# A scale column made by two-column matmuls, and transposes moved ahead of it, in front of a V projection

## The chip, the cores and the metric

The kernel runs on one core of a Trainium2 chip. The metric is the device time of one execution in microseconds (us). The profile's span, from the first to the last profiled instruction, is 1.8 to 2.3 us shorter than that time; what lies outside it varies from run to run.

## The reference

The kernel is the attention half of a two-stream transformer block: batch 2, 256 image and 32 text tokens, width 1152. What matters here is the way to the image stream's V:

```python
mod_i = (silu(c) @ wmod_img).reshape(B, 6, 1, D)
shi, sci, gai = mod_i[:, 0], mod_i[:, 1], mod_i[:, 2]
hi = layernorm(x_img) * (1 + sci) + shi
qkvi = hi @ wqkv_img            # q, k, v of the image stream
# ... text stream, softmax attention, output projections, gates ...
```

The kernel applies the scale `1 + sci` first, computes V from the scaled input and adds the shift's share later. So before the first V matmul it needs normalised x, transposed (contraction on the partitions), and the scale as a column per 128 channels. The 256 image tokens of a batch are two token tiles of 128: tiles 0 and 1 of batch 0, 2 and 3 of batch 1.

## The kernel before

The contraction is cut into nine blocks of 128 (`kt` 0 to 8). The scale needs all nine rows of blocks of its weights, which arrive in four transfers (kt 0-3, 4-6, 7, 8), before any column of it is complete. The code is cut, and the arguments of DVE's instructions are shortened.

```python
def sc_rows(r0, r1):            # scale as rows: silu(c) is stationary, weights stream
    ...                         # r0 == 0: the constant 1, by `unit` and `warm`
    for kt in range(r0, r1):
        for g in range(NGG):    # four column tiles of the array side by side
            mm(sc_ps[LW*g:LW*g+LW], lhsT=sT32[:, kt, :], rhs=group(w_sc_i, kt, g),
               start=False, stop=(kt == KT-1), tile_position=(0, LW*g))

def sc_cols(c0, c1):            # rows to columns: a transpose on DVE
    nc.vector.transpose(sc1_i[:, c0:c1, :], sc_ps[:, c0:c1, :])

def x_scale(k0, k1, b, step=TPB):   # hS = xT * column, on DVE
    ...

# the order in front of V (cut)
for out in [x_transposes(k0, 0) for k0 in (0, 3, 6)]:
    out()                       # batch 0: transpose on TensorE, copy out of PSUM
sc_rows(0, 4)
warm_up(3)
sc_rows(4, 7)
out01 = x_transposes(0, 1)      # batch 1, channel groups 0 and 3
out31 = x_transposes(3, 1)
sc_rows(7, K8)
sc_rows(K8, KT)
out61 = x_transposes(6, 1)      # group 6
out01()
sc_cols(0, 1)
x_scale(0, 1, 0, step=1)
sc_cols(1, 5)
x_scale(1, 3, 0)
v_open(A0, 0, 3)                # the first V matmuls
```

Two pools of PSUM, into which the kernel's matmuls write, matter. A pool hands out its banks in turn, and a tile that gets a used bank waits until the earlier contents have been read. `ps_tr` has two banks for transposes: groups 0 and 3 of batch 0 take them first, and groups 0 and 3 of batch 1 need the same two again. `ps_mm` has six.

## Time and profile before

| | kernel before |
|---|---|
| time, median of the first 3 runs | 118.11 us |
| span of the profiled run | 116.0 us |
| TensorE busy | 95% of the span |
| first V matmul starts | 14.15 us |
| from there to the end | 101.85 us |

The page's first part gives busy time by engine, the chain of work that ended last tells what the end waited for, step by step back to the start, and the timeline gives start and duration of each group. A bracket at the end of a timeline row gives the engine's idle time before it and what ended that. A landing is the moment at which a transfer's data have arrived. The prediction shows the lines and reads them.

### The profile page before, as it was taken

Reading aid. Unit: us, or ns where it says so; the run is one execution under the profiler, and the core shown is the slowest. Engines: PE = TensorE matmul, PEld = TensorE weight load, DVE = VectorE, ACT = ScalarE, POOL = GpSimd, SP = SyncE. Lnnn points to the kernel's source line nnn. Section 1 sums busy time; section 2 is a strip of 40 time slices with the busy share of each in tenths; the row PEclk is TensorE's granted clock in tenths of the full one; section 3 lists DMA queues with packets and bytes.
Section 4 is the critical chain, followed back from the end, with each engine's and each line's share of the span. In section 5 each row is a group of like instructions: output and inputs, shape, how many; then the busy total and the mean of one; then the engine's idle time right before and its main releaser. Section 6 shows DMA issues by size and latency. Waiting matters only on the chain.

```text
span 116.0 us, 2561 instructions
## 1 busy us (share of the span) xinstructions
PE 110.5 (95%) x1064; PEld 63.6 (55%) x1072; DVE 72.2 (62%) x153; ACT 44.3 (38%) x92; POOL 12.4 (11%) x34
## 2 busy tenths in 40 slices
PE   4999999999999999999999999999999999999990
PEld 1246644445674444444454457887866565566670
DVE  3478594062869999999995040018758508566571
ACT  4799710041752298725241233244657400100000
POOL 7300000000000000000000000003440700407000
PEclk9999999999999999999999999999999999999999
DMA  3999999999999999999999999999999999931323
GB/s 111 373 373 404 406 405 408 416 411 408 416 398 408 319 408 410 405 412 412 411 340 412 412 412 414 402 416 400 412 403 409 409 415 366 363 139 37 116 51 102
DMA packets 18917, 41.02 MB, mean 354 GB/s; under 512 B 1323, under 2 KB 1851, under 8 KB 18907
## 3 DMA queue, kind: packets, MB, share of 16 engines
q1 hardware_dynamic: 18032, 39.85, 89.4%
q0 software_dynamic: 480, 0.89, 2.3%
q10 hardware_dynamic: 395, 0.12, 0.4%
q8 instruction: 8, 0.13, 0.4%
q14 instruction: 2, 0.02, 0.0%
HBM read 39.52 MB, written 1.34 MB: 352 GB/s over the span
## 4 chain that ended last, share of the span: by engine, by line
PE 84%; DMA 8%; DVE 2%; SPq 1%; issue 1%; ACT 1%; DVEq 0%
PE ps L61 52%; PE vps L61 15%; DMA t<-in_wmod_img_dram 8%; PE gps L61 5%; PE aps L61 5%; PE sps L61 4%; DVE tmp L701 1%; PE sc_ps L61 1%; DVE o L702 1%; SPq L104 1%; PE tp L64 1%; ACT pT L621 1%; PE pT_ps L64 0%; SPq L108 0%; PE tpt L64 0%
## 5 line engine op out<-in xcount | busy, mean ns | idle before, releaser
L61 PE MATMUL ps<-xT_i,t 128*128 128x512 bf16 x157 | 35.4, 379 | 0.3
L61 PEld LDWEIGHTS <-t 128*128 128x128 bf16 x324 | 20.5, 98 | 19.0 <-issue 0.5
L435 DVE SCALAR_TENSOR_TENSOR acc_sh<-t,sTf,acc_sh 128x1152 f32<-128x1152 bf16 x16 | 21.4, 1404 | 0.0
L61 PE MATMUL ps<-t,aT 128*128 128x384 bf16 (+3 forms) x153 | 20.3, 308 | 0.0
L61 PE MATMUL vps<-t,hS_i 128*128 128x512 bf16 (+1 forms) x106 | 17.8, 325 | 0.2
L61 PEld LDWEIGHTS <-aT 128*128 128x128 bf16 (+1 forms) x153 | 13.0, 101 | 7.1 <-issue 0.8
L61 PEld LDWEIGHTS <-hS_i 128*128 128x128 bf16 x108 | 9.0, 98 | 8.7 <-DVE hS_i L264 0.4
L365 ACT CAST qkT<-ps 128x512 bf16<-128x512 f32 (+2 forms) x11 | 6.1, 551 | 15.0 <-PE ps L61 13.6
L701 DVE TENSOR_TENSOR tmp<-ps,gb 128x384 bf16<-128x384 f32 (+2 forms) x13 | 6.8, 524 | 7.2 <-DMA gb<-mod_scratch 3.8
L587 POOL TENSOR_SCALAR pb<-e,rs 128x32 bf16<-128x32 f32 (+1 forms) x5 | 2.2, 445 | 76.0 <-DVE rs L584 76.0
L61 PE MATMUL wps<-warm 128*128 128x512 bf16 x24 | 8.1, 499 | 1.6 <-DVE unit L127 1.5
L363 ACT ACTIVATE qkT<-ps 128x512 bf16<-128x512 f32 (+2 forms) x11 | 6.1, 561 | 8.6 <-PE ps L61 8.5
L180 DVE CAST v_i<-vps 128x512 bf16<-128x512 f32 x5 | 3.5, 691 | 7.5 <-PE vps L61 7.5
L572 DVE TENSOR_REDUCE nmx<-sps 128x1 f32<-128x288 f32 x4 | 1.8, 458 | 9.5 <-PE sps L61 9.5
L182 ACT CAST v_i<-vps 128x512 bf16<-128x512 f32 x4 | 2.3, 580 | 9.9 <-PE vps L61 9.9
L61 PEld LDWEIGHTS <-sT 128*32 128x32 bf16 x180 | 4.6, 96 | 2.4 <-issue 1.8
L61 PEld LDWEIGHTS <-warm 128*128 128x128 bf16 x25 | 2.7, 118 | 5.5 <-issue 3.0
L634 DVE TENSOR_SCALAR aT<-aps,svc 128x288 bf16<-128x288 f32 x9 | 4.3, 518 | 2.2 <-PE aps L61 2.2
L61 PE MATMUL sps<-qkT 128*128 128x288 bf16 (+1 forms) x54 | 5.3, 287 | 0.0
L61 PE MATMUL gps<-t,sT 128*32 128x288 bf16 x144 | 5.2, 287 | 0.0
L61 PE MATMUL ps<-hT_t,t 128*128 128x64 bf16 x162 | 5.2, 193 | 0.0
L61 PE MATMUL aps<-pT,v_i 128*128 128x288 bf16 x36 | 5.1, 287 | 0.1
(111 smaller groups left out, 105.3 us busy)
## 6 DMA issues: line engine op xcount, KB each, us to landing
t<-in_wqkv_txt_dram SPq DMA_DIRECT2D x3, 2592.0 KB, 19.1
t<-in_wmod_img_dram SPq DMA_DIRECT2D x2, 2592.0 KB, 14.1
t<-in_wmod_txt_dram SPq DMA_DIRECT2D x2, 2592.0 KB, 18.1
t<-in_wqkv_img_dram SPq DMA_DIRECT2D x3, 864.0 KB, 14.0
t<-in_wqkv_img_dram SPq DMA_DIRECT2D x1, 2592.0 KB
t<-in_wo_img_dram SPq DMA_DIRECT2D x3, 864.0 KB, 9.8
t<-in_wqkv_img_dram SPq DMA_DIRECT2D x3, 576.0 KB, 10.0
t<-in_wmod_txt_dram SPq DMA_DIRECT2D x2, 864.0 KB, 13.1
```

Source lines behind the costliest of these rows:

```text
L61: return pin(nc.tensor.matmul(*a, **k))
L64: return pin(nc.tensor.transpose(*a, **k))
L104: nc.sync.dma_start(x_i[:, b * TPB:(b + 1) * TPB, :], x_img[b].rearrange("(p t) d -> p t d", t=TPB))
L180: nc.vector.tensor_copy(out_ap, in_ap)
L182: nc.scalar.copy(out_ap, in_ap)
L363: nc.scalar.mul(out_ap, in_ap, SCALE)
L365: nc.scalar.copy(out_ap, in_ap)
L435: pin(nc.vector.scalar_tensor_tensor(acc, w_sh_t[:, kt, :], col, acc, op0=ALU.mult, op1=ALU.add))
L572: pin(nc.vector.reduce_max(nmx[0:qn, :], sps[0:qn, :], axis=AX.X, negate=True))
L587: pin(nc.gpsimd.tensor_scalar(pb[0:qn, NI + 2 * NT:NI + 3 * NT], e[0:qn, NI:NTOK], rs[0:qn, :], 0.0, op0=ALU.mult, op1=ALU.add))
L634: nc.vector.tensor_scalar(dst, tiles[(b, dt)][:], bias, None, op0=ALU.add)
L701: nc.vector.tensor_mul(tmp[:, 0:n], ps[:, 0:n], gb[:, b, c0:c0 + n])
```

## The change

The intent: the first block's scale column shouldn't have to go through rows and a DVE transpose. With the weights as the stationary operand, nine matmuls of two columns make it in place in PSUM, and DVE multiplies straight from there. The transposes of batch 1 are started earlier, by token tile, and the k0 = 6 groups of both batches have banks reserved. The diff is cut at the marks.

```diff
+    sc0_ps = ps_mm.tile([P, B], f32, tag="mm")
+    tp60 = ps_mm.tile([P, 3, NI], bf, tag="mm", name="tp")
+    tp61 = ps_mm.tile([P, 3, NI], bf, tag="mm", name="tp")
     sc_ps = ps_mm.tile([P, KT, LW], f32, tag="mm")
+    def sc_first(r0, r1):
+        if r0 == 0:
+            mm(sc0_ps[:], lhsT=warm[:, 0:P], rhs=unit[:, 0:B], start=True, stop=False)
+        for kt in range(r0, r1):
+            mm(sc0_ps[:], lhsT=w_sc_i[:, kt, 0:P], rhs=sT[:, kt, :], start=False, stop=(kt == KT - 1))
...
+    def x_tiles(k0, b):
+        return (tp61 if b else tp60) if k0 == 6 else ps_tr.tile([P, 3, NI], bf, tag="tr", name="tp")
...
...
     sc_rows(0, 4)
-    warm_up(3)
+    sc_first(0, 4)
+    warm_up(2)
+    t0, t3, t6 = [(x_tiles(k0, 1), k0, 1) for k0 in (0, 3, 6)]
+    x_transposes(*t0, ts=(1,))
+    x_transposes(*t3, ts=(1,))
     sc_rows(4, 7)
-    out01 = x_transposes(0, 1)
-    out31 = x_transposes(3, 1)
-    sc_rows(7, K8)
-    sc_rows(K8, KT)
-    out61 = x_transposes(6, 1)
-    out01()
-    sc_cols(0, 1)
-    x_scale(0, 1, 0, step=1)
-    sc_cols(1, 5)
+    sc_first(4, 7)
+    x_transposes(*t0, ts=(0,))
+    x_transposes(*t3, ts=(0,))
+    x_transposes(*t6)
+    sc_first(7, K8)
+    sc_first(K8, KT)
+    sc_rows(7, KT)
+    x_out(*t0)
+    x_out(*t6)
+    x_scale(0, 1, 0, step=1, first=True)
+    sc_cols(0, 5)
     x_scale(1, 3, 0)
     v_open(A0, 0, 3)
...
```

More of the change, by code (lines that the diff above doesn't have):

```diff
@@ L238, in sc_rows, with x_transposes, x_out @@
                    start=False, stop=(kt == KT - 1), tile_position=(0, LW * g))
-    def x_transposes(k0, b):
-        tr_pool = b == 1 or k0 < 6
-        tp = (ps_tr if tr_pool else ps_mm).tile([P, 3, NI], bf, tag="tr" if tr_pool else "mm", name="tp")
+    def x_tiles(k0, b):
+        return (tp61 if b else tp60) if k0 == 6 else ps_tr.tile([P, 3, NI], bf, tag="tr", name="tp")
+    def x_transposes(tp, k0, b, ts=range(TPB)):
         for kt in range(k0, k0 + 3):
-            for t in range(TPB):
+            for t in ts:
                 i = b * TPB + t
                 tr(tp[:, kt - k0, t * P:(t + 1) * P], xn_i[:, i, kt * P:(kt + 1) * P], ident[:])
+    def x_out(tp, k0, b):
         dst = xT_i[:, k0:k0 + 3, b * NI:(b + 1) * NI]
-        def copy_out():
-            pin(nc.vector.tensor_copy(dst, tp[:]) if k0 == 3 else nc.scalar.copy(dst, tp[:]))
-        return copy_out
+        pin(nc.vector.tensor_copy(dst, tp[:]) if k0 == 3 else nc.scalar.copy(dst, tp[:]))
     sc1_i = const.tile([P, KT, LW], f32, name="scc", tag="scc")
@@ L258, in sc_cols, with x_scale @@
                                 sc_ps[:, c0:c1, :].rearrange("p c l -> p (c l)")))
-    def x_scale(k0, k1, b, step=TPB):
+    def x_scale(k0, k1, b, step=TPB, first=False):
         for kt in range(k0, k1):
@@ L263, in x_scale @@
                 t0, t1 = b * NI + t * P, b * NI + (t + step) * P
-                pin(nc.vector.tensor_scalar(hS_i[:, kt, t0:t1], xT_i[:, kt, t0:t1], sc1_i[:, kt, b:b + 1], None,
+                pin(nc.vector.tensor_scalar(hS_i[:, kt, t0:t1], xT_i[:, kt, t0:t1],
+                                            sc0_ps[:, b:b + 1] if first else sc1_i[:, kt, b:b + 1], None,
                                             op0=ALU.mult))
@@ L302 @@
     ln_norm(x_i[:, 2, :], s2[:, 0:1], r2, P, xn_i[:, 2, :])
-    for out in [x_transposes(k0, 0) for k0 in (0, 3, 6)]:
-        out()
-    sc_rows(0, 4)
-    warm_up(3)
-    sc_rows(4, 7)
-    out01 = x_transposes(0, 1)
-    out31 = x_transposes(3, 1)
-    sc_rows(7, K8)
-    sc_rows(K8, KT)
-    out61 = x_transposes(6, 1)
-    out01()
-    sc_cols(0, 1)
-    x_scale(0, 1, 0, step=1)
-    sc_cols(1, 5)
+    tps = [(x_tiles(k0, 0), k0, 0) for k0 in (0, 3, 6)]
+    for tp in tps:
+        x_transposes(*tp)
+    for tp in tps:
+        x_out(*tp)
+    sc_rows(0, 4)
+    sc_first(0, 4)
[3 more added lines that the diff above has]
+    x_transposes(*t3, ts=(1,))
+    sc_rows(4, 7)
+    sc_first(4, 7)
[9 more added lines that the diff above has]
+    sc_cols(0, 5)
     x_scale(1, 3, 0)
     v_open(A0, 0, 3)
-    out31()
-    out61()
+    x_out(*t3)
     x_scale(0, 3, 1)
```

## The prediction

> **What bounds the kernel now.** I read the page's busy shares first, then the chain of work that ended last, then the timeline of the start, engine by engine.
>
> From the page of the kernel before:
>
> ```profile
> PE 110.5 (95%) x1064; PEld 63.6 (55%) x1072; DVE 72.2 (62%) x153; ACT 44.3 (38%) x92; POOL 12.4 (11%) x34
> ...
> PEclk9999999999999999999999999999999999999999
> ...
> PE 84%; DMA 8%; DVE 2%; SPq 1%; issue 1%; ACT 1%; DVEq 0%
> ```
>
> TensorE is busy 95% of the span at full clock and holds 84% of the chain. The chain in order of time shows where it is not yet the bound:
>
> ```profile
> 2.12 9.54 DMA t<-in_wmod_img_dram
> ...
> 11.70 0.55 PE sc_ps L61 x12
> 12.25 0.78 PE tp L64 x12
> 13.03 0.46 PE sc_ps L61 x8
> ...
> 13.51 0.23 DVE scc L257
> ...
> 13.83 0.27 DVE hS_i L264
> ...
> 14.15 2.12 PE vps L61 x9
> ```
>
> Until 11.7 us the start waits for the scale weights. Then come the last scale rows, the transposes of batch 1, the scale column made by DVE, the first scaled block, and at 14.15 us the first V matmul. From there to 111.4 us the chain is TensorE throughout, but for 0.65 us of one ScalarE copy and gaps of about 0.05 us (some of those are lost records: the spacing there is twice the usual 0.216 us). So the time follows the start of the first V matmul, one to one. Everything that the change touches lies in front of it.
>
> The parts of the timeline that I use, TensorE first (start, duration, both us):
>
> ```profile
> 10.10 0.66 PE L61 MATMUL sc_ps<-t,sT 128*32 128x288 bf16 x16
> ...
> 10.92 0.59 PE L61 MATMUL wps<-warm 128*128 128x512 bf16 x2 [0.16 <-issue]
> 11.70 0.55 PE L61 MATMUL sc_ps<-t,sT 128*32 128x288 bf16 x12 [0.18 <-DMA t<-in_wmod_img_dram]
> 12.19 0.84 PE L64 MATMUL tp<-ident,xn_i 128*128 128x128 bf16 x12
> 12.96 0.51 PE L61 MATMUL sc_ps<-t,sT 128*32 128x288 bf16 x8
> 13.58 0.49 PE L64 MATMUL tp<-ident,xn_i 128*128 128x128 bf16 x6
> ```
>
> ScalarE and DVE in the same stretch:
>
> ```profile
> 11.14 1.48 ACT L250 COPY xT_i<-tp 128x768 bf16<-128x768 bf16 x2
> ...
> 11.34 0.57 DVE L212 TENSOR_SCALAR xn_i<-x_i,sm,rstd 128x1152 bf16<-128x1152 bf16 x1
> 11.83 0.55 DVE L250 COPY xT_i<-tp 128x768 bf16<-128x768 bf16 x1
> 13.51 0.22 DVE L257 STREAM_TRANSPOSE scc<-sc_ps 128x32 f32<-128x32 f32 x1 [1.13 <-PE sc_ps L61]
> 13.83 0.42 DVE L264 TENSOR_SCALAR hS_i<-xT_i,scc 128x128 bf16<-128x128 bf16 x2
> ```
>
> The reader is to see three things. Transposes come every 0.056 us: (0.84 - 0.22) / 11. A group of four column-tiled row matmuls comes every 0.121 us (x16 are four groups). And the two banks of the transposing pool come free only when their batch-0 contents are copied out: the first at 11.14 + 0.78 = 11.92 us (ScalarE), the second at 11.83 + 0.55 = 12.38 us (DVE).
>
> **What the Trainium skill says.** "TensorEngine Tiling (Array Packing)", Key Properties: changing the tiling mode drains the engine. The trace agrees and gives the price: from the start of the last column-tiled matmul to the next full-width load it takes 0.21 us, where a group costs 0.12; from the last full-width transpose to the next column-tiled one 0.15 us, where a transpose costs 0.056. So about 0.09 us a switch. "TensorE: Matmul & The Clock Gate", Part 3, The mechanism: weight loads may be pulled ahead, matmuls keep their order. The trace agrees: the transposes at 13.58 us wait for ScalarE's third copy, and no matmul behind them passes. "VectorE: DVE Perf Modes", Why PSUM operands drop a tier: an operand in PSUM caps the DVE at its 2x mode. Whether that holds for a one-column scalar no row of the kernel before shows; it would turn 128 elements at 0.25 us into some 0.28 (estimate, from the 0.033 us that the trace has between the 128- and the 256-element scaling).
>
> **The change part by part.**
>
> *Removed:* the 32-column DVE transpose (0.22 us) and the wait between it and the scaling; 13.51 to 13.83 is 0.32 us of the chain. One of three warm-up matmuls (0.216 us) goes too, but it lay in front of a wait for weights.
>
> *Added:* ten matmuls of 2 columns (one for the constant, nine for the rows), each with a full load of 128 weights. The nearest thing in the trace is the text block's 128x64 matmul, also with a new load each: 33 take 1.12 us and one 0.193, so they start every 0.029 us and end 0.19 after their start. Ten cost 0.3 us of issue. The scale column for kt = 0 is ready 0.19 us after the last of them, instead of 0.30 + 0.32 after the last row group.
>
> *What the data allows:* the last row of scale weights is there at 13.13 us (its matmul starts at 13.157). Then 0.03 issue, 0.19 matmul, 0.05 signal, 0.27 scaling, 0.06 signal: V could start at 13.75. The first V weights, issued at 3.74 and landing 10.1 us later, come at 13.83. So the intent is worth at most 14.15 - 13.86 = 0.29 us, 0.25% of 118.1.
>
> *What the order makes of it:* the built program shows TensorE's new sequence: 16 row matmuls, 5 small, 2 warm-up, 3 transposes of token tile 3 into the first pool bank, **3 transposes of token tile 3 into the second pool bank**, 12 row matmuls (kt 4-6), 3 small, 12 transposes, 2 small, 8 row matmuls, V. The transposes come in front of the row matmuls now, and the second three still wait for DVE's copy that ends at 12.38. Only the k0 = 6 groups have banks of their own; the groups 0 and 3 do not. I step through it:
>
> - last of the 16 row matmuls starts 10.48; +0.21 switch: 10.70; 5 small to 10.85; 2 warm-up to 11.28.
> - token tile 3 is normalised at 11.43, but the first bank is free at 11.92, seen at 11.97: three transposes to 12.13.
> - second bank free at 12.38, seen at 12.44: three transposes, the last starts 12.55. In the kernel before, the 12 row matmuls had been issued by 12.09 and half of all transposes by this time.
> - +0.15 switch: 12.70, three groups, the last starts 12.95; +0.21: 13.16, 3 small to 13.25.
> - 12 transposes: 13.25 + 12 x 0.056 = 13.92.
> - 2 small at 13.92 and 13.95; their weights (12.4 and 13.13) are long there. The last ends at 14.14.
> - DVE: +0.04 signal, a second wait of some 0.07 (13.73 to 13.83 held such a pair): 14.25; scaling 0.25 to 0.30: 14.50 to 14.55; +0.06: **V at 14.56 to 14.61**, say 14.58.
>
> TensorE meanwhile: switch, 8 row matmuls from about 14.10, back in full mode by 14.42, so it then waits for DVE, not DVE for it.
>
> *Behind it:* DVE's transpose of five blocks is one instruction of about 0.34 us (32 columns take 0.22, 128 take 0.31). It starts at about 14.60, so the second scaled block is there at about 15.25, and V's second step needs it at 14.58 + 4 x 0.216 = 15.44. Batch 1 scales at about 15.9 to 16.5, needed at 14.58 + 12 x 0.216 = 17.2. V's weight blocks are all there before. So no new stall follows and the shift stays rigid: 14.58 - 14.15 = +0.43 us, and 118.11 + 0.43 = **118.5 us**.
>
> **The rivals.**
>
> 1. *The intent comes true:* V starts with its weights at 13.86, giving 117.8 us. For it: the removed DVE step really is in the chain. Against it: the column now waits for 12 transposes that used to be elsewhere, and for the second bank. It would need the three early transposes not to wait for 12.38. I give it about one chance in eight, or some middle result that cannot be told from no change.
> 2. *Clock:* TensorE idles from 11.28 to 11.97 and from 12.13 to 12.44 with one warm-up fewer. If the granted clock dropped, the next microseconds would run slower and the time would rise to 119.5 or more. Against it: the kernel before idles about as much in total between 11.3 and 14.15, in more pieces, and its clock row is full in every slice. About 4%.
> 3. *Hidden anyway:* later waits for weights could swallow the shift. Against it: the chain has no transfer after 11.66 us. If it held, 118.1.
> 4. *DVE becomes the bound:* a scalar read from PSUM makes both halves slow, say 0.4 us each. V would start 0.1 to 0.15 later, 118.7.
>
> **Range and chances.** The steps carry an error of some 0.15 us, mostly in the signals and in the scaling from PSUM; runs of the kernel before spread over 117.92 to 118.4. So 118.1 to 118.9 should hold it 8 times in 10. All rivals but a lasting clock drop stay within 2% (2.4 us). Faster by over 2%: 0.005; within 2%: 0.985; slower by over 2%: 0.01.
>
> **What would show it right or wrong.** In the changed kernel's timeline: the transposes of token tile 3 split in two threes, at about 11.97 and 12.44; the row matmuls kt 4-6 start at about 12.7 instead of 11.70, with no wait for the weights; 12 transposes in a row from about 13.25 to 13.9; the first scaling on DVE at about 14.25 and the first V matmul at about 14.58, after a wait for DVE. The chain would go through the DVE copy of 11.83 and then through TensorE's transposes, no longer through the weights. The prediction is wrong if the row matmuls still start near 11.70, if the small matmuls take much more than 0.03 us each, if V starts before 14.15, or if the span after V is not 101.85 us as before (116.0 - 14.15).

## The result, and the profile after

The changed kernel took 118.62 us (median of 6 runs, 118.48 to 118.72) against 118.31 us (6 runs, 117.92 to 118.45) for the kernel before. The ratio is 1.0032, 95% interval 1.0014 to 1.0049. A ratio here is the mean time of one kernel's runs over that of the other's runs of the same rounds, so it is not quite the ratio of the medians. The change costs some 0.3 us, well within 2%.

The chain of the changed kernel in order of time, cut to the stretch in front of V (start us, duration us, what):

```profile
11.05 1.07 DVE xn_i L212 x2
12.13 0.48 DVE xT_i L260
...
12.64 0.33 PE tp L64 x3
12.97 0.64 PE sc_ps L61 x15
13.61 0.69 PE tp L64 x12
14.31 0.06 PE sc_ps L61 x2
...
14.46 0.27 DVE hS_i L272
...
14.78 1.25 PE vps L61 x5
```

The weights of the scale, which led the chain before, are gone from it. It now comes from layer norm on DVE, goes through DVE's copy out of the second transposing bank (`xT_i L260`), and only when that ends do three transposes, twelve row matmuls, three small ones, twelve transposes and two small ones follow each other on TensorE.

TensorE's timeline of the changed kernel (start, duration):

```profile
12.18 0.80 PE L64 MATMUL tp<-ident,xn_i 128*128 128x128 bf16 x6 [0.76 <-DVE xn_i L212]
12.90 0.55 PE L61 MATMUL sc_ps<-t,sT 128*32 128x288 bf16 x12
13.39 0.23 PE L61 MATMUL sc_ps<-sT,t 128*128 128x2 bf16 x3
13.48 0.83 PE L64 MATMUL tp<-ident,xn_i 128*128 128x128 bf16 x12
...
14.78 1.25 PE L61 MATMUL vps<-t,hS_i 128*128 128x512 bf16 x5
```

and DVE's:

```profile
12.04 0.55 DVE L260 COPY xT_i<-tp 128x768 bf16<-128x768 bf16 x1
14.46 0.42 DVE L272 TENSOR_SCALAR hS_i<-xT_i,sc_ps 128x128 bf16<-128x128 bf16 x2 [1.87 <-PE sc_ps L61]
```

The reader is to see the row `x6` at 12.18: six transposes take 0.80 us where six in a row take 0.49, because the second three start at 12.65, 0.05 us after DVE's copy ended at 12.04 + 0.55 = 12.59. The row matmuls of kt 4-6, which ran at 11.70 before, follow at 12.90, although the queue that loads weights saw theirs landed at 12.02. (The releaser in brackets, `DVE xn_i L212`, is the normalising of the other token tile, which happened to end at 12.13 too. The tile that the first three need was normalised at 11.63; what ended their wait is ScalarE's copy out of their bank, which also ended at 12.13. In e9 and e11 the profile names that copy.)

From the first V matmul to the end it is 101.71 us, before 101.85. So the loss lies wholly in front of V, as the starts have it: 14.78 against 14.15.

### The profile page after: what moved, and what is told of

The parts are those of the page before. It is cut to its first block, busy times and chain, and to the rows that moved or that the text cites. A ratio compares the mean times of both kernels' runs of the same rounds, so it can differ in the third digit from the quotient of the medians.

```text
span 116.5 us, 2577 instructions
## 1 busy us (share of the span) xinstructions
PE 110.3 (95%) x1072; PEld 63.5 (55%) x1081; DVE 72.0 (62%) x152; ACT 44.2 (38%) x92; POOL 12.4 (11%) x34
## 4 chain that ended last, share of the span: by engine, by line
PE 84%; ACT 5%; DMA 3%; DVE 3%; issue 1%; DVEq 0%
PE ps L61 52%; PE vps L61 15%; PE gps L61 5%; PE aps L61 5%; PE sps L61 4%; DMA x_i<-in_x_img_dram 3%; ACT xn_i L197 2%; ACT xn_i L198 2%; DVE tmp L718 1%; DVE xn_i L212 1%; PE tp L64 1%; DVE o L719 1%; PE sc_ps L61 1%; ACT pT L638 1%; ACT rstd L207 1%
## 5 line engine op out<-in xcount | busy, mean ns | idle before, releaser
L61 PE MATMUL wps<-warm 128*128 128x512 bf16 x23 | 7.6, 491 | 1.5 <-DVE unit L127 1.5
```

The lines of the kernel that those rows point to most:

```text
L61: return pin(nc.tensor.matmul(*a, **k))
```

## The experiments

The landings of the transfers shift from execution to execution. In the twelve profiles the second half of x lands between 5.66 and 6.15 us, the last row of scale weights is seen between 12.44 and 13.82 us, the first V weights land between 13.19 and 14.49 us. A single profile's V start therefore says little by itself; I read it against the landing that released it. For sizes I use the ratio and the difference of the mean spans, which leaves out the varying time outside the span.

**e1_small_only.** The small matmuls alone; order and banks of the kernel before. The diff is against the kernel before and shortened, as in the next ones.

```diff
     sc_rows(0, 4)
+    sc_first(0, 4)
     warm_up(3)
     sc_rows(4, 7)
+    sc_first(4, 7)
     # groups 0 and 3 of batch 1, all token tiles, in the two-bank pool
-    sc_rows(7, K8); sc_rows(K8, KT)
+    sc_first(7, K8); sc_first(K8, KT)
+    sc_rows(7, KT)
     # group 6 of batch 1, in the two-bank pool
-    sc_cols(0, 1); x_scale(0, 1, 0, step=1); sc_cols(1, 5)
+    x_scale(0, 1, 0, step=1, first=True); sc_cols(0, 5)
```

> The small column matmuls alone, with the transposes in the order and the banks of the kernel before. Theory (the order of the transposes and the wait for the second pool bank cost the time, the small matmuls save some): rows kt 4-6 start near 11.70 us as before, the small matmuls of kt 7 and 8 near 13.15, the first scaling on DVE near 13.45 instead of 13.83, V at about 13.95 (the six transposes of group 6 still wait for ScalarE and now end last), so -0.2 us, ratio 0.998 to before. Rival (ten small matmuls with two more mode switches cost more than they save): V at or after 14.5, ratio 1.003 or more.

Measured: 117.81 us, ratio 0.9971 (0.9936 to 1.0005), mean span 0.34 us below the kernel before. The interval just includes 1, but the rival's 1.003 is far outside it. TensorE's timeline:

```profile
11.41 0.55 PE L61 MATMUL sc_ps<-t,sT 128*32 128x288 bf16 x12
...
13.37 0.49 PE L64 MATMUL tp<-ident,xn_i 128*128 128x128 bf16 x6 [0.17 <-ACT xT_i L259]
13.70 2.54 PE L61 MATMUL vps<-t,hS_i 128*128 128x512 bf16 x11
```

In this execution the weights came early: the rows of kt 4-6 start at 11.41 instead of 11.70, so of the 0.45 us by which V is earlier than before only some 0.16 us belong to the change (an estimate: from the start of those rows to V it is 2.29 us, before 2.45). V starts behind the six transposes of group 6, which wait for ScalarE's copy, as expected; DVE had its first block scaled at 13.21. The small matmuls don't cost the time; they point to a small gain.

**e2_order_only.** The new order and banks alone; the column by DVE as before.

```diff
     # from the changed kernel
-    sc_first(...)                                   # all four calls
-    x_scale(0, 1, 0, step=1, first=True); sc_cols(0, 5)
+    sc_cols(0, 1); x_scale(0, 1, 0, step=1); sc_cols(1, 5)
```

> The new order and the new banks alone, the column made by DVE's transpose as before. Theory: the first transposes at about 11.97 and 12.44, rows kt 4-6 from 12.7, twelve transposes to 13.9, rows kt 7-8 to 14.3, DVE transpose at 14.4, scaling at 14.7, V at about 15.0: +0.85 us, ratio 1.007, so slower than the whole change. Rival (the small matmuls cost the time): no slower than before, ratio 1.000 or less.

Measured: 118.89 us, ratio 1.0055 (1.0027 to 1.0084), mean span +0.79 us. This is slower than the whole change. Its chain goes the same way:

```profile
11.68 0.48 DVE xT_i L260
...
12.20 0.33 PE tp L64 x3
12.53 0.48 PE sc_ps L61 x12
13.01 0.78 PE tp L64 x12
...
14.20 0.23 DVE scc L265
```

The two parts add up: -0.34 (small matmuls) + 0.79 (order) = +0.45 us, and the whole change has +0.34 to +0.38 us of mean span in its two later series. The order is what costs.

**e3_free_banks.** The changed kernel with its order, but groups 0 and 3 of batch 1 get the reserved banks, and group 6 of batch 1 takes the pool.

```diff
-    tp61 = ps_mm.tile(...)
+    tp01 = ps_mm.tile(...)
+    tp31 = ps_mm.tile(...)
...
-        return (tp61 if b else tp60) if k0 == 6 else ps_tr.tile(...)
+        own = {(6, 0): tp60, (0, 1): tp01, (3, 1): tp31}
+        return own[k0, b] if (k0, b) in own else ps_tr.tile(...)
```

> The whole change with its order, but groups 0 and 3 of batch 1 have the banks of their own and group 6 takes the pool. Theory: six transposes of token tile 3 in one row at about 11.5, before the weights of kt 4-6, rows kt 4-6 from about 11.95, V at 13.85 to 13.95 with its weights as the last wait: -0.25 us, ratio 0.998 to before. Rival of the added work: as the whole change, V at 14.6 to 14.8, ratio 1.003.

Measured: 118.25 us, ratio 0.9992 (0.9962 to 1.0022), mean span -0.11 us: no gain to be told, and the loss isn't seen. (Its interval overlaps that of the changed kernel, 1.0014 to 1.0049, a little, so the timeline has to carry the reading.) TensorE's timeline:

```profile
11.21 0.51 PE L64 MATMUL tp<-ident,xn_i 128*128 128x128 bf16 x6 [0.27 <-DVE xn_i L212]
11.65 0.55 PE L61 MATMUL sc_ps<-t,sT 128*32 128x288 bf16 x12
13.95 2.32 PE L61 MATMUL vps<-t,hS_i 128*128 128x512 bf16 x10 [0.29 <-DVE hS_i L274]
```

The six early transposes start 0.05 us after their token tile is normalised (10.58 + 0.58 = 11.16) and take 0.51 us instead of 0.80. So the same order without the wait for banks is harmless. The second half of x landed at 5.66 here, the earliest of the twelve; counted from that landing V starts after 8.29 us, where the changed kernel takes 8.72. V starts 0.14 us after its weights landed (13.81), while its first scaled block was there at 13.66: in this execution the weights were the last wait. The six spans spread from 115.6 to 116.5 us; whether the weights cause that no second profile shows.

**e5_rows_first.** The changed kernel with its banks, but the rows and small matmuls of kt 4-6 in front of all transposes of batch 1.

```diff
-    x_transposes(*t0, ts=(1,))
-    x_transposes(*t3, ts=(1,))
     sc_rows(4, 7)
     sc_first(4, 7)
+    x_transposes(*t0, ts=(1,))
+    x_transposes(*t3, ts=(1,))
     x_transposes(*t0, ts=(0,))
```

> The whole change with its banks, but rows and small matmuls of kt 4-6 stand in front of all transposes of batch 1 again. Theory: rows at 11.70, 18 transposes from 12.3 to 13.3 with no wait for a bank, the last small matmul at 13.3, scaling at 13.6, V at about 13.9: -0.25 us, ratio 0.998. Rival of the added work: ratio 1.003 as the whole change. If the weights of V were the bound in any order, no kernel of this set starts V before 13.83 us or gains more than 0.3 us.

Measured: 117.69 us, ratio 0.9957 (0.9931 to 0.9983), mean span -0.27 us. TensorE's timeline:

```profile
11.88 0.55 PE L61 MATMUL sc_ps<-t,sT 128*32 128x288 bf16 x12 [0.41 <-DMA t<-in_wmod_img_dram]
12.46 1.23 PE L64 MATMUL tp<-ident,xn_i 128*128 128x128 bf16 x18
14.16 2.12 PE L61 MATMUL vps<-t,hS_i 128*128 128x512 bf16 x9
```

The rows wait for their weights again and for nothing else, and eighteen transposes follow in one row of 1.23 us. The wait for the second bank has not gone: DVE's copy ends at 12.64 and the fourth transpose starts 0.05 us later, at 12.69, where without it 12.62 was due. But only 0.07 us are lost on it, and the rows are no longer behind it. V starts 0.16 us after its weights (14.00), and right after DVE's scaling. (13.83, named in the expectation, is no fixed floor: e1 started V at 13.70, with weights that had landed at 13.19.)

**e9_after_again.** The changed kernel once more, beside the next three.

> The changed kernel once more, so that it stands beside the others on the same chip. Both theories: ratio 1.003 to before, V at 14.6 to 14.8 us.

Measured: 118.53 us against 118.26, ratio 1.0018 (0.9997 to 1.0038), mean span +0.38 us, V at 14.81. The loss is smaller in this ratio and the interval touches 1; the spans have it in full.

**e6_second_three_late.** The changed kernel with only the second early three behind the rows.

```diff
     x_transposes(*t0, ts=(1,))
-    x_transposes(*t3, ts=(1,))
     sc_rows(4, 7)
     sc_first(4, 7)
+    x_transposes(*t3, ts=(1,))
     x_transposes(*t0, ts=(0,))
```

> The whole change, but the second three early transposes (those that wait for DVE's copy of the second pool bank) stand behind the rows and small matmuls of kt 4-6; the first three stay in front. Theory (the wait for the second bank is the largest part of the loss): rows kt 4-6 at about 12.25 instead of 12.9, V at about 14.25 to 14.4, some 0.35 us less than the whole change, ratio 1.000 to 1.001 to before. Rival (moving transposes in front of the rows costs by itself, whatever they wait for): ratio 1.003 as the whole change.

Measured: 118.47 us (5 runs), ratio 1.0013 (0.9998 to 1.0027), mean span +0.09 us where the changed kernel has +0.38 in the same rounds. TensorE's timeline:

```profile
12.27 0.33 PE L64 MATMUL tp<-ident,xn_i 128*128 128x128 bf16 x3 [0.76 <-ACT xT_i L260]
12.52 0.55 PE L61 MATMUL sc_ps<-t,sT 128*32 128x288 bf16 x12
```

Beside the repeated changed kernel, whose rows start at 12.94 with the same landing of x (6.15 here, 6.11 there), the rows start 0.42 us earlier, and V at 14.56 instead of 14.81. That V gains only 0.25 us has a plain reason: fifteen transposes now follow the rows instead of twelve, three of 0.056 us more. V's weights landed at 14.49, but the chain has V behind DVE's scaling. By the times alone this run can't be told from the changed kernel; by the spans and the timeline taking the second three out of the way of the rows is worth some 0.3 us, the larger part of the loss (six spans of 116.5 to 116.8 against five of 116.2 to 116.4).

**e4_delay.** The kernel before with four warm-up matmuls right in front of V, to see whether a late V shows in full at the end.

```diff
+    warm_up(4)
     v_open(A0, 0, 3)
```

> The kernel before with four 512-column warm-up matmuls right in front of V. If the time follows the start of V one to one, V moves from 14.15 to about 14.8 (13.92 + 4 x 0.216) and the time by +0.6 us, ratio 1.005, with the span after the start of V unchanged at about 101.8 us. If later waits swallow a late start, the span after V shrinks and the ratio stays at 1.000 to 1.002.

Measured: 118.48 us, ratio 1.0011 (0.9986 to 1.0035), mean span +0.41 us. TensorE's timeline:

```profile
13.77 0.49 PE L64 MATMUL tp<-ident,xn_i 128*128 128x128 bf16 x6
14.10 1.03 PE L61 MATMUL wps<-warm 128*128 128x512 bf16 x4
14.97 1.24 PE L61 MATMUL vps<-t,hS_i 128*128 128x512 bf16 x5
```

Within this execution the delay is as expected: DVE had the first block at 14.28, so V could have started at 14.34 and started at 14.97, 0.63 us later, and from there to the end it is 101.70 us, as elsewhere. The rest swallows nothing. But the expected ratio of 1.005 was missed, and 1.0011 lies where the expectation put the other case, so what speaks for one to one is the constant rest and not this time. The six spans run from 116.0 to 117.0 us. Here V waits for the transposes and ScalarE instead of for DVE's column, so how much of the delay is a delay depends on the landings of the execution. How the 0.2 us that is missing in the mean divides between this and chance I can't say.

**e8_small_before_six.** As e5_rows_first, with the small matmuls of kt 7 and 8 in front of group 6. (Groups 0 and 3 are each transposed whole, not by token tile; the diff leaves that out.)

```diff
-    x_transposes(*t6)
     sc_first(7, K8)
     sc_first(K8, KT)
+    x_transposes(*t6)
     sc_rows(7, KT)
```

> As the kernel with the rows first, and the small matmuls of kt 7 and 8 in front of the six transposes of group 6, so that DVE can scale while they run. Theory with the weights of V as the floor: the first scaling up to 0.3 us earlier, TensorE comes free for V at about the same time, V at most 0.13 us earlier (it started 0.16 after its weights had landed, the least seen is 0.14), ratio 0.995 to 0.996, not to be told from rows first. If the weights of V are no floor: V 0.2 to 0.3 us earlier, ratio 0.993.

Measured: 118.13 us, ratio 0.9976 (0.9949 to 1.0003), mean span -0.24 us: not to be told from rows first. DVE began to scale 0.53 us ahead of V (13.47 against 14.00), and V still started only 0.17 us after its weights landed (13.84); the chain has it directly behind the rows of kt 7-8. In none of the twelve profiles does V start before its first weights have landed; the least distance is 0.07 us (e6).

**e10_rows_first_again and e11_after_third.** The first is e5_rows_first once more, the second the changed kernel a third time, in the same rounds, to see whether the reordered version beats both.

> The kernel with the rows first once more, in the same rounds as the changed kernel, to see whether it beats both. If the order is the cause of the loss: ratio 0.995 to 0.998 to before, spans near 115.9 us. If its first result was luck with the launch: ratio 1.000.

> The changed kernel a third time, beside it: ratio 1.002 to 1.003 to before, spans near 116.5 us, so 0.5 to 0.7 us above the kernel with the rows first.

Measured: rows first 118.16 us, ratio 1.0001 (0.9978 to 1.0024); the changed kernel 118.65 us, ratio 1.0032 (1.0018 to 1.0046), mean span +0.34. Against the changed kernel the reordered one is 0.3% faster here (1.0001 over 1.0032), as the theory wants, though the two intervals overlap a little and one of its six runs (118.91 us) is slower than all of the changed kernel's. Against the kernel before, its first series showed -0.4% and this one nothing; two of its six spans here are 116.6 and 116.7 us, the others 115.8 to 116.1. The two series ran on different chips (number 15 in the record, and 6). So it beats the changed kernel in the mean ratio of each, and whether it beats the kernel before stays open.

The second profile of rows first shows what its order removes and what it doesn't. Its chain in order of time:

```profile
12.11 0.48 DVE xT_i L260
...
12.63 1.00 PE tp L64 x15
...
14.10 1.25 PE vps L61 x5
```

The weights came early (rows at 11.34), the second half of x landed at 6.06 as in the first profile of the changed kernel, and the fourth transpose waited 0.30 us for DVE's copy of the second bank, about as long as in the changed kernel. Yet V starts at 14.10 and not at 14.78. From the end of that copy to V it is 1.52 us in both profiles of rows first, and 2.18 to 2.19 us in all three of the changed kernel. So both hang on the second bank; what rows first saves is 0.66 us of rows, small matmuls and switches between them that the changed kernel lets queue behind it.

The changed kernel's third profile is the best test of the prediction's arithmetic, because the second half of x landed at 5.91 us in it, as in the execution that the prediction was read from (5.89). Its chain in order of time (start us, duration us, what):

```profile
11.93 0.48 DVE xT_i L260
...
12.45 0.33 PE tp L64 x3
...
14.26 0.27 DVE hS_i L272
...
14.58 1.25 PE vps L61 x5
```

The second three transposes start at 12.45 (predicted 12.44), the scaling at 14.26 (14.25), V at 14.58 (14.58). The last row of scale weights had been seen at 13.82 only in this execution, later than in any other of the changed kernel, and it moved nothing: V starts 8.72, 8.71 and 8.67 us after the second half of x landed in the three profiles of this kernel. Its start hangs on x, no longer on the scale's weights. (The first V weights, landed at 14.49, were 0.09 us ahead of it.)

## Why the prediction was right

**What bounds the kernel.** Right. The rest after V is 101.70 to 101.92 us in all twelve profiles, also where V starts 0.8 us later than before (e4_delay).

**The removed step.** Right in kind: e1_small_only shows the small column path to be no loss, -0.34 us in mean span where I had -0.2.

**The order.** Right, and it is the step on which the sign hangs. The first three transposes came at 12.18, the second at 12.65, the rows at 12.90, the twelve transposes at 13.48, the scaling at 14.46, V at 14.78, each 0.20 to 0.23 us after the predicted moment. The common part is the landing of x, 0.17 us later in that execution than in the one that I had read (6.06 against 5.89); no step between had an error over 0.03 us; in the third profile, with x landing as assumed, every moment is met within 0.03 us. e3_free_banks shows the bank wait as the cause by taking it away with the order kept, e6_second_three_late the share of the second bank, e5_rows_first and its repeat that with the rows in front the loss isn't seen (0.9957 and 1.0001), and e2_order_only that the order alone costs more than the whole change.

**The size.** Right in direction, a little large: +0.43 us was predicted, the three series give 1.0032, 1.0018 and 1.0032, or 0.2 to 0.4 us, and +0.34 to +0.38 us of mean span in the two series that list both kernels' spans. The term that was mis-sized is the start of V in the kernel before. I took 14.15 from one execution with a span of 115.99 us; the mean of that kernel's spans in three sets of 11 runs is 116.15 to 116.19. So its typical V starts some 0.15 to 0.2 us later (an estimate from the spans), and the loss against it is that much smaller. The changed kernel, whose chain no longer starts at the scale weights, doesn't share this spread: its 18 spans lie between 116.3 and 116.8.

**The rivals.** The intent didn't come true, for the reason given. The clock stayed: 0.996 to 1.000 in the 18 runs of the changed kernel, 0.995 to 1.000 in those of the kernel before. The reason given for that was weak: by the busy time of the profile, TensorE was idle for 0.37 us between 11.3 and 14.15 in the kernel before and for 0.98 us between 11.3 and 14.78 in the changed one, so not about as much. A scalar in PSUM doesn't make DVE the bound: the two scalings took 0.258 and 0.252 us, before 0.254 and 0.248 from SBUF. "Hidden anyway" did not hold for the loss; a gain it can hide, as in e3_free_banks, where V's own weights were the last wait.

## What to carry to other kernels

A step moved earlier in an in-order queue brings its waits along, and everything behind it pays for them. Before moving one, ask what it waits for at the new place, buffers included: here three transposes of 0.17 us held twelve ready matmuls for their PSUM bank. Where the wait can't be removed, put ready work in front of it: rows first still waits for the bank, but no longer has the rows behind it. And read a start that hangs on transfers from several executions, since one profile shows one draw of the landings.

## What the Trainium skill lacked or had wrong

- "TensorEngine Tiling (Array Packing)", Key Properties, says that a change of tiling mode drains the engine, but not what that costs, and no other page does. Here the next full-width load follows the start of the last column-tiled 288-column matmul after 0.21 us (a group lasts 0.12), and the next column-tiled matmul follows the last full-width transpose after 0.15 us (one lasts 0.056).
- "VectorE: DVE Perf Modes", Why PSUM operands drop a tier, has any PSUM operand cap the mode. A one-column scalar in PSUM doesn't show it: 0.258 and 0.252 us for 128 elements, against 0.254 and 0.248 with the scalar in SBUF.
- "TensorE: Matmul & The Clock Gate", Back-to-back issue gap, gives about 81 ns for 128 and 131 ns for 512 columns in streams with a new weight load each, and keeps some 56 and 216 ns for isolated matmuls. Here transposes of 128 columns with a load each start every 56 ns, and V matmuls of 512 columns every 216 ns; the two-column matmuls of this change, with a load of 128 weights each, start every 25 to 39 ns.
